# LayerNorm outputs of a fused attention and MLP block transposed by the DMA engine and modulated in place, instead of on TensorE through PSUM

One core of one Trainium2 chip. The metric is device time of one execution in microseconds (us), lower is better.

## The reference

One transformer block with adaptive modulation, bf16, 2048 tokens of 640 features, 32 heads of 20 features, MLP width 1536. Cut to what matters:

```python
mod = (silu(c) @ w_mod).reshape(1, 6, 1, 640)
sa, ca, ga, sb, cb, gb = (mod[:, i] for i in range(6))
h = layernorm(x) * (1 + ca) + sa            # "modulation"
qkv = h @ wqkv                              # ... split in 32 heads
p = softmax(q @ k.T * 20 ** -0.5)           # 2048 x 2048 for each head
x = x + ga * ((p @ v) @ wo)
h = layernorm(x) * (1 + cb) + sb
x = x + gb * (((h @ w_gate) * (h @ w_up)) @ w_down)
```

LayerNorm works on tokens in partitions, the matmuls after it need features in partitions. So each normalised tile (128 tokens x 640) has to be transposed. The scale and shift of the modulation are per feature, so after the transpose they are per partition, which one instruction does for 512 tokens.

## The kernel before

All engines' work is created as tasks with an assumed duration in ns, and a planner in the program puts them into one fixed order per engine before anything runs. `dve(195, ...)` is a VectorE task assumed to take 195 ns. `prio` is its rank among tasks that are ready in the plan (lower goes first), `dma("sp", bytes, ...)` is an entry of the one DMA queue on SyncE. At run time each engine does its list in order and waits where it must.

First LayerNorm, block `tc` of 512 tokens. Four TensorE transposes fill a PSUM bank, one eviction modulates 512 tokens of 128 features:

```python
def hT_rounds(tc, prio):
    ...
    for k in range(KD):                      # KD = 5 groups of 128 features
        mms = []
        for i in range(4):                   # 4 tiles of 128 tokens
            f = lambda e, b, i=i, k=k: e.transpose(bankh(b)[:, i * 128:(i + 1) * 128],
                                                   xn[:, s2, i, k * 128:(k + 1) * 128], ident[:])
            mms.append((C128, f))
        def after(r, k=k):                   # eviction with modulation, DVE or ACT
            ...
            f = lambda e: e.tensor_scalar(dst, bankh(r.b["b"])[:, 0:512], mcol[:, 1, k:k + 1], mcol[:, 0, k:k + 1],
                                          op0=ALU.mult, op1=ALU.add)
            return [evac(512, 455, f, fa, [r.last] + ev_col)]
        ...
```

The second LayerNorm does the same for each chunk of tokens (`h2T`, in the "suffix": output projection, LayerNorm, MLP) beside the attention of later chunks. The modulation columns are made from 25 matmuls for each vector, each one column wide:

```python
f = lambda e, b, nbk=nbk, k=k: e.matmul(ps[:, b, nbk:nbk + 1], buf[:, k, nbk * 128:(nbk + 1) * 128],
                                        scol[:, k:k + 1], start=(k == 0), stop=(k == KD - 1))
```

The exponentials run on ScalarE (line 1214) and VectorE makes the rest of the weights by adding integer constants to a linear score (`DB`, line 1238, then the shifts `DSS`, line 1252). These shifts feed the p @ v matmuls:

```python
tsx = Task("dve", 575.0, fsh, list(st_["p1"]), prio=2.5 + .001 * qi, name=f"SH.{qi}.{jj}")
```

Keys and queries reach their final layout by a round trip over the same SyncE queue: written to DRAM rows (`k_rows<-KPA`, `q_rows<-KPA`), with zeros written between the query rows (`q_rows<-Ocp`), and read back (`KT<-k_rows`, `QT<-q_rows`).

```python
q_zero[tc] = [dma("sp", 12 * H * 1024, lambda e, tc=tc: e.dma_start(..., Ocp[48:80, 1, KD - 1, :]...),
                  [z_oc[1], d_wm[4][0]], prio=9.5, dur=720.0, gate=WM_GATE + 20 + 12 * tc)]
```

The softmax here doesn't subtract the row's maximum and nothing guards it: scores larger than these inputs give would overflow.

## Time and profile before

| | before |
|---|---|
| time | 869.9 us, median of 2 (869.32 to 870.48) |
| span of the profiled run | 865.9 us, granted clock 0.992 |
| exponentials | 691, 788.3 us of ACT |
| first exponential starts, last ends | 17.28, 829.0 us |
| idle of ACT between exponentials | 23.4 us in all |
| of it in front of exponentials 1 to 10, 11 to 20, 21 to 59, 60 to 690 | 6.6, 6.3, 5.8, 4.8 us |

How to read it: exponentials are numbered from 0 in order of time. "The stall in front of exponential n" is the time from the end of exponential n-1 to the start of exponential n in the trace's records of ACT. ACT is the bound, so the time of a kernel is nearly first start + 788 us + stalls + tail, and each change can be looked for in one of these four terms. "Half clock" is time in which the granted clock of TensorE is recorded as 0.5. The prediction below shows the lines of the profile.

### The profile page before, as it was taken

How to read it: one execution, taken by the hardware profiler on the slowest of the kernel's cores; microseconds unless marked ns; L12 is line 12 of the kernel's file. 1: busy time of each engine (PE TensorE's matmuls, PEld its weight loads, DVE VectorE, ACT ScalarE, POOL GpSimd, SP SyncE). 2: the span in 40 equal slices, each digit the busy share in tenths (PEclk: the TensorE clock that was granted, in tenths of full speed). 3: DMA queues.
4: the chain of work that ended last, by engine and by line, in shares of the span. 5: the costliest groups of instructions: out<-in, count | busy, mean ns of one | idle time of the engine just before them, and what ended most of it. 6: DMA issues, size and time to landing. Idle time of an engine off the chain costs nothing.

```text
span 865.9 us, 30616 instructions
## 1 busy us (share of the span) xinstructions
PE 829.4 (96%) x13568; PEld 327.5 (38%) x13568; DVE 713.1 (82%) x1338; ACT 802.5 (93%) x718; POOL 32.0 (4%) x65
## 2 busy tenths in 40 slices
PE   8899999999999999999999999999999999999998
PEld 4433333322233322233333322223445444455577
DVE  7865888796999999999889999999779877775463
ACT  4698999999999999899999999999999999999931
POOL 2300000000001000000000100000001100000000
PEclk9997999999999999999999999999999999999999
DMA  9163331122510125110301011110310036203640
GB/s 300 38 216 94 92 86 37 29 71 76 156 29 23 33 55 146 43 24 6 66 10 44 5 36 44 44 36 2 67 50 7 21 75 139 59 21 82 136 88 18
DMA packets 118459, 56.37 MB, mean 65 GB/s; under 512 B 84439, under 2 KB 118327, under 8 KB 118327
## 3 DMA queue, kind: packets, MB, share of 16 engines
q1 hardware_dynamic: 117399, 53.26, 24.2%
q8 instruction: 107, 1.75, 0.9%
q10 hardware_dynamic: 928, 1.15, 0.4%
q14 instruction: 25, 0.20, 0.1%
HBM read 42.93 MB, written 9.16 MB: 60 GB/s over the span
## 4 chain that ended last, share of the span: by engine, by line
PE 44%; ACT 34%; DVE 15%; issue 3%; DMA 2%; POOL 1%; SPq 1%; DVEq 0%; ACTq 0%
ACT PP L1214 34%; PE ps_all L747 16%; PE ps_all L1596 13%; PE ps_all L1180 12%; DVE DB L1238 4%; DVE DSS L1252 3%; PE ps_all L914 2%; DVE st L802 1%; DMA k_rows<-KPA 1%; DVE st L1400 1%; DVE xck L1390 1%; DVE OT L1305 1%; DVE xn L1407 1%; PE ps_all L829 1%; DMA stg<-in_B_w_gate_dram 1%
## 5 line engine op out<-in xcount | busy, mean ns | idle before, releaser
L1214 ACT ACTIVATE PP<-ps_all 128x1536 bf16<-128x1536 f32 (+1 forms) x691 | 788.3, 1279 | 13.5 <-PE ps_all L1180 9.7
L1180 PE MATMUL ps_all<-QT,KT 32*128 32x512 bf16 (+1 forms) x2560 | 295.2, 341 | 14.5 <-ACT PP L1214 11.5
L1252 DVE TENSOR_SCALAR DSS<-DB 128x2048 int16<-128x2048 int16 x400 | 265.9, 683 | 20.0 <-PE ps_all L1596 17.7
L1238 DVE TENSOR_SCALAR DB<-ps_all 128x512 int16<-128x512 f32 x320 | 217.2, 682 | 38.7 <-PE ps_all L1180 37.0
L1180 PEld LDWEIGHTS ps_all<-QT,KT 32*128 32x128 bf16 x2560 | 77.2, 91 | 256.6 <-ACT PP L1214 185.7
L1596 PE MATMUL ps_all<-PP,Vf 128*32 128x512 bf16 (+3 forms) x2184 | 171.9, 344 | 1.5 <-DVE OT L1305 1.5
L1596 PE MATMUL ps_all<-DSS,Vf 128*32 128x512 bf16 (+2 forms) x1880 | 151.7, 351 | 0.0
L747 PE MATMUL ps_all<-h2T,stg 128*32 128x512 bf16 x1440 | 109.7, 381 | 2.8 <-DVE DB L1238 1.7
L1596 PEld LDWEIGHTS ps_all<-PP,Vf 128*32 128x32 bf16 (+1 forms) x2184 | 48.3, 94 | 95.3 <-issue 84.9
L1596 PEld LDWEIGHTS ps_all<-DSS,Vf 128*32 128x32 bf16 (+1 forms) x1880 | 47.8, 96 | 36.1 <-issue 16.0
L747 PE MATMUL ps_all<-wd,hprod 128*32 128x320 bf16 x1152 | 55.2, 300 | 0.4 <-DVE DB L1238 0.3
L747 PEld LDWEIGHTS ps_all<-h2T,stg 128*32 128x32 bf16 x1440 | 34.8, 96 | 35.1 <-issue 9.4
L1465 DVE CAST gsb<-ps_all 128x512 bf16<-128x512 f32 (+1 forms) x48 | 29.5, 615 | 10.8 <-PE ps_all L747 10.6
L747 PEld LDWEIGHTS ps_all<-wd,hprod 128*32 128x32 bf16 x1152 | 29.2, 96 | 14.9 <-issue 4.8
L747 PE MATMUL ps_all<-wV,hT 128*32 128x320 bf16 x640 | 32.9, 300 | 1.9 <-DVE DB L1238 0.8
L1403 POOL TENSOR_SCALAR sd<-mv 128x1 f32<-128x1 f32 x14 | 7.0, 499 | 739.7 <-DVE mv L1402 739.7
L747 PE MATMUL ps_all<-wo,Ocp 128*32 128x320 bf16 x640 | 31.9, 300 | 0.4 <-DVE xck L1390 0.3
L1596 PE MATMUL ps_all<-DB,Vf 128*32 128x512 bf16 (+2 forms) x376 | 32.1, 349 | 0.0
L1305 DVE STREAM_TRANSPOSE OT<-ps_all 128x512 f32<-128x512 f32 (+1 forms) x40 | 24.2, 605 | 8.8 <-PE ps_all L1596 8.6
L914 PE MATMUL ps_all<-hT,wk 128*32 128x512 bf16 x380 | 29.9, 381 | 0.4 <-DVE Vf L994 0.4
L914 PE MATMUL ps_all<-hT,wq 128*32 128x512 bf16 x375 | 29.0, 394 | 0.9 <-DVE Vf L994 0.3
L1476 DVE TENSOR_TENSOR hprod<-ps_all,gsb 128x512 bf16<-128x512 f32 x36 | 24.5, 681 | 5.3 <-PE ps_all L747 5.3
(107 smaller groups left out, 486.6 us busy)
## 6 DMA issues: line engine op xcount, KB each, us to landing
stg<-in_B_w_gate_dram SPq DMA_DIRECT2D x50, 160.0 KB
stg<-in_B_w_up_dram SPq DMA_DIRECT2D x50, 160.0 KB
KT<-k_rows SPq DMA_DIRECT2D x120, 32.0 KB
QT<-q_rows SPq DMA_DIRECT2D x22, 128.0 KB
wm<-in_w_mod_dram SPq DMA_DIRECT2D x3, 800.0 KB
k_rows<-KPA SPq DMA_DIRECT2D x18, 128.0 KB
x<-in_A_x_dram SPq DMA_DIRECT2D x7, 320.0 KB
xck<-in_A_x_dram SPq DMA_DIRECT2D x3, 640.0 KB
```

The source lines that it names most:

```text
L747: return lambda e, b: e.matmul(ps[32 * x:32 * x + 32, b, 0:n], lhs()[:, 32 * x:32 * x + 32], rhs(), tile_position=(0, 32 * x), start=st, s ...
L802: bns.append(dve(393, lambda e, t=t, i=i, hf=hf: e.bn_stats(st[:, i, 6 * hf:6 * hf + 6], x0[:, t, 320 * hf:320 * hf + 320]), [d_x[tc][i // ...
L829: f = lambda e, b, i=i, k=k: e.transpose(bankh(b)[:, i * 128:(i + 1) * 128], xn[:, s2, i, k * 128:(k + 1) * 128], ident[:])
L914: f = [lambda e, b_, k=k, x=x: e.matmul(ps[x:x + min(32, w - x), b_, :], wx[:, k, r0 + x:r0 + min(x + 32, w)], hT[tc][:, k, :], tile_posit ...
L1180: ems.append(lambda e, i=i, kt=kt: e.matmul(dstf()[:, i * u.n:(i + 1) * u.n], KT[32 * u.s:32 * u.s + 32, u.j, kt * 128:(kt + 1) * 128], QT ...
L1214: return e.activation(PPs[g % 2][:, cellp["p"], 0:nu * 512], ps[:, b0:b0 + nu, :].rearrange("p b c -> p (b c)"), AFT.Exp, scale=ESCALE)
L1238: return e.tensor_scalar(DB0[:, st_["slot"], x * 512:(x + 1) * 512], bank(cell["b"]), EBIAS, 0.0, op0=ALU.add, op1=ALU.max)
L1252: return e.tensor_scalar(DSS[:, cell["s"], :], DB0[:, st_["slot"], :], float(SHIFTS[jj]), None, op0=ALU.add)
L1305: t1 = Task("dve", n * 1.1 + 70, lambda e: e.transpose(OT[:, 0:n], ps[:, BPV, 0:n]), [], prio=0.0, name=f"T1.{it}")
L1465: f = lambda e: e.tensor_copy(gsb[:, gs, 0:n], ps[:, r.b["b"], 0:n])
L1476: f = lambda e: e.tensor_tensor(hprod[:, fc, 0:n], ps[:, r.b["b"], 0:n], gsb[:, gs, 0:n], ALU.mult)
L1596: ems.append(lambda e, i=i, kt=kt, stt=stt, stp=stp: e.matmul(ps[32 * s:32 * s + mc, BPV, 0:u.n], Vf[:, (kt * H + 4 * u.j + s) * VW:(kt * ...
```

## The change

Intent: take 130 transposes and 35 PSUM evictions off TensorE, VectorE and ScalarE by letting 26 DMA transposes write the transposed tile straight to SBUF, and modulate it there in place. Apart from that the column matmuls are written 64 wide, so that TensorE looks busier and its clock stays up. Block 0 and the last chunk stay on TensorE.

```diff
+DMA_T = (1, 2, 3)
+TR_BYTES = 300000
...
-                f = lambda e, b, nbk=nbk, k=k: e.matmul(ps[:, b, nbk:nbk + 1], ...
-                                                        scol[:, k:k + 1], ...
+                f = lambda e, b, nbk=nbk, k=k: e.matmul(ps[:, b, nbk * NCOL:nbk * NCOL + NCOL], ...   # NCOL = 64
+                                                        scol[:, k:k + 1].to_broadcast([128, NCOL]), ...
...
+        if tc in DMA_T:
+            for i in range(4):
+                tr_last[tc].append(dma("sp", TR_BYTES, lambda e, i=i: e.dma_start(
+                    hT[tc][:, :, i * 128:(i + 1) * 128], xn[:, s2, i, :], transpose=True), [t_xn[tc][i]], prio=0.05,
+                    dur=550.0))
+            for k in range(KD):
+                t_hT[tc].append(dve(195, lambda e, k=k: e.tensor_scalar(
+                    hT[tc][:, k, :], hT[tc][:, k, :], mcol[:, 1, k:k + 1], mcol[:, 0, k:k + 1], op0=ALU.mult,
+                    op1=ALU.add), tr_last[tc] + ev_col, prio=1))
+            return
...
+        if not tail:
+            for tl in range(ntl):
+                tr_l.append(dma("sp", TR_BYTES, lambda e, tl=tl: e.dma_start(
+                    h2T[:, :, tl * 128:(tl + 1) * 128], xn2[:, tl, :], transpose=True), ..., prio=0.05, dur=550.0))
+            for k in range(KD):
+                t_h2.append(dve(n * .265 + 60, ... in place on h2T[:, k, 0:n] ...,
+                    tr_l + [r_sb.evac[0], r_cb.evac[0]], prio=1))
-        for k in range(KD):
+        for k in range(KD if tail else 0):
...
-            sc.activity(start, 1.0 if cand.name[:3] == "col" else cand.dur * 2.37)
+            sc.activity(start, cand.dur * 2.37)
```

`dur=550.0` is the assumed time that one transpose holds the SyncE queue.

More of the change, by code (lines that the diff above doesn't have):

```diff
@@ L749, in quarters @@
         return [one(x) for x in range(4)]
-    C512, C320, C128, C1 = 216.0, 136.0, 57.0, 26.0
+    C512, C320, C128, C1 = 216.0, 136.0, 57.0, 28.0
+    NCOL = 64
     def X(n):
@@ L760, in col_round, with src @@
             for k in range(KD):
-                f = lambda e, b, nbk=nbk, k=k: e.matmul(ps[:, b, nbk:nbk + 1], buf[:, k, nbk * 128:(nbk + 1) * 128],
-                                                        scol[:, k:k + 1], start=(k == 0), stop=(k == KD - 1))
+                f = lambda e, b, nbk=nbk, k=k: e.matmul(ps[:, b, nbk * NCOL:nbk * NCOL + NCOL],
+                                                        buf[:, k, nbk * 128:(nbk + 1) * 128],
+                                                        scol[:, k:k + 1].to_broadcast([128, NCOL]),
+                                                        start=(k == 0), stop=(k == KD - 1))
                 mms.append((C1, f))
+        def src(r):
+            return ps[:, r.b["b"], 0:KD * NCOL].rearrange("p (a b) -> p a b", b=NCOL)[:, :, 0]
         def after(r):
             if plus:
-                f = lambda e: e.tensor_scalar(mcol[:, slot, :], ps[:, r.b["b"], 0:KD], 1.0, None, op0=ALU.add)
+                f = lambda e: e.tensor_scalar(mcol[:, slot, :], src(r), 1.0, None, op0=ALU.add)
             else:
-                f = lambda e: e.tensor_copy(mcol[:, slot, :], ps[:, r.b["b"], 0:KD])
+                f = lambda e: e.tensor_copy(mcol[:, slot, :], src(r))
             return [dve(75, f, [r.last], prio=0)]
@@ L1414, in suffix @@
         tr_l = []
-        for k in range(KD):
+        if not tail:
+            for tl in range(ntl):
+                tr_l.append(dma("sp", TR_BYTES, lambda e, tl=tl: e.dma_start(
+                    h2T[:, :, tl * 128:(tl + 1) * 128], xn2[:, tl, :], transpose=True),
+                    [t_xn2[tl]] + (first if alt else bd.get("h2T", []) + kv_last), prio=0.05, dur=550.0))
+            for k in range(KD):
+                t_h2.append(dve(n * .265 + 60, lambda e, k=k: e.tensor_scalar(
+                    h2T[:, k, 0:n], h2T[:, k, 0:n], mcol[:, 3, k:k + 1], mcol[:, 2, k:k + 1], op0=ALU.mult, op1=ALU.add),
+                    tr_l + [r_sb.evac[0], r_cb.evac[0]], prio=1))
+        for k in range(KD if tail else 0):
             mms = []
@@ L1506, in suffix @@
         bd["hp"] = dn_last[-1:]
-        bd["tr"] = tr_l[-1:]
+        bd["tr"] = tr_l if not tail else tr_l[-1:]
         bd["out"] = outs
```

## The prediction

> **What bounds the kernel now.** I began with the page's busy shares, then cut the span into stages by what ScalarE (ACT) does, and only then looked at the clock, the groups and the chain of waits.
>
> ```profile
> PE 829.4 (96%) x13568; PEld 327.5 (38%) x13568; DVE 713.1 (82%) x1338; ACT 802.5 (93%) x718; POOL 32.0 (4%) x65
> ```
>
> PE looks fullest, but a matmul's recorded time overlaps its neighbours', so 96% does not make PE the bound. ACT's 802.5 us are nearly all the exponentials of line 1214 (691 of them, 788.3 us), and the change removes none. So the useful question is where ACT is not running exponentials. The busy times in stretches that I cut at the first exponential (17.28), at two stalls and at the last exponential (829):
>
> ```profile
> core 0: us, PE busy (x) PEld busy (x) DVE busy (x) ACT busy (x) POOL busy (x), PEclk, DMA share, GB/s
> 0.00:17.28 17.28, 13.72 (x159) 6.89 (x163) 12.91 (x52) 5.11 (x9) 3.96 (x13) 0.90 0.97 303
> 17.28:50.00 32.72, 29.59 (x481) 13.61 (x473) 27.34 (x71) 24.70 (x25) 9.79 (x22) 1.00 0.31 89
> 50.00:77.00 27.00, 25.31 (x374) 8.62 (x372) 19.75 (x34) 26.36 (x23) 0.00 (x0) 1.00 0.59 178
> 77.00:90.00 13.00, 12.29 (x150) 4.43 (x153) 2.40 (x7) 7.66 (x7) 0.00 (x0) 0.61 0.40 102
> 90.00:829.00 739.00, 715.91 (x11402) 266.73 (x11394) 633.12 (x1133) 734.23 (x645) 16.98 (x28) 1.00 0.23 55
> 829.00:866.00 37.00, 32.60 (x1020) 27.27 (x1020) 17.54 (x45) 4.47 (x12) 1.23 (x2) 1.00 0.12 33
> ```
>
> Read the ACT column against the length of the row. From 90 to 829 us ACT idles 739.00 - 734.23 = 4.8 us: 85% of the kernel is bound by ACT and cannot give more than that. What can move is the head (17.28 us to the first exponential), 8.0 us of idleness in 17.28 to 50, 5.3 us in 77 to 90, and the tail of 37 us, which PE bounds. The granted clock in 77 to 90 is 0.61; in finer stretches:
>
> ```profile
> 10.00:11.00 1.00, 1.00 (x9) 0.76 (x9) 0.35 (x3) 0.00 (x0) 0.00 (x0) 0.50 1.08 344
> 11.00:12.00 1.00, 1.00 (x12) 1.00 (x11) 0.69 (x2) 0.67 (x1) 0.00 (x0) 0.50 1.15 310
> ...
> 76.00:78.00 2.00, 0.69 (x16) 0.43 (x16) 1.07 (x2) 0.99 (x2) 0.00 (x0) 0.95 0.23 56
> 78.00:80.00 2.00, 2.00 (x17) 0.41 (x14) 0.68 (x1) 1.45 (x1) 0.00 (x0) 0.50 0.24 73
> 80.00:82.00 2.00, 2.00 (x33) 0.95 (x32) 0.17 (x2) 1.11 (x2) 0.00 (x0) 0.50 0.95 191
> ```
>
> PE ran at half clock twice: about 9.8 to 12.9 us, and about 77.9 to 88.9 us. Both times the one-column matmuls of line 761 (the modulation columns) ran just before or during it, at 7.7 to 9.9 and at 75.9 to 83. The groups that the change touches:
>
> ```profile
> L829 PE MATMUL ps_all<-ident,xn 128*128 128x128 bf16 x80 | 7.9, 244 | 1.8 <-DVE hT L837 1.1 <-ACT hT L835 0.6
> L837 DVE TENSOR_SCALAR hT<-ps_all,mcol 128x512 bf16<-128x512 bf16 x14 | 7.4, 541 | 2.4 <-PE ps_all L829 2.3
> L835 ACT ACTIVATE hT<-ps_all,mcol 128x512 bf16<-128x512 bf16 x6 | 4.7, 778 | 8.8 <-PE ps_all L829 8.7
> L1423 DVE TENSOR_SCALAR h2T<-ps_all,mcol 128x512 bf16<-128x512 bf16 x15 | 7.7, 530 | 0.7 <-PE ps_all L1418 0.7
> L813 DVE TENSOR_SCALAR xn<-x,mv,rs 128x640 bf16<-128x640 bf16 x16 | 6.9, 433 | 0.6 <-POOL rs L811 0.5
> ```
>
> The reader should see small groups: the whole transposing path is some 30 us of work spread over three engines.
>
> **What the Trainium skill says.** (1) "VectorE: DVE Perf Modes", the perf-mode tier table: a tensor_scalar on bf16 in SBUF may run at four elements a cycle, with PSUM as source at no more than two. The trace agrees in part: line 1252 (128x2048, int16, SBUF) took 683 ns, near the fast rate, but line 813 (128x640, bf16, two per-partition scalars) took 433 ns, which fits two a cycle as well. (2) The same page, "The three transpose paths": 390 ns for a 128x128 transpose on TensorE, 1309 ns on the DMA. Here a TensorE transpose is recorded at 219 ns and a group of four occupies 0.33 us start to start. (3) "Advanced Engine Details and Errata", X-Bar Transpose: such transfers are as fast as plain ones, 350 to 400 GB/s. By (3) the 164 KB of one transfer take 0.45 us, by (2) its five blocks take 6.5 us; no run yet says which, and this is the largest doubt. (4) "TensorE: Matmul & The Clock Gate", Part 1: the clock is halved after a window of about 3.4 us with too little activity. The trace agrees: the first slow spell is 3.1 us long, the second 11 us, three such windows.
>
> **The change, part by part.**
> - Removed on PE: 60 of line 829's 80 transposes (block 0 keeps 20) and 70 of the suffixes' 80 (the last chunk keeps 10). 130 x 82 ns = 10.7 us, with 35 rounds fewer on the two PSUM banks that projections, suffix and DVE scores share. In 90 to 829 this lies beside ACT's exponentials and is worth almost nothing.
> - Removed evictions: block 0 used 3 of line 837's 14 and 2 of line 835's 6, so 11 on DVE and 4 on ACT go, with 15 + 5 of line 1423. DVE: 11 x 541 + 15 x 530 + 5 x 391 ns = 15.9 us. ACT: 4 x 778 ns = 3.1 us, but those four stand where ACT was waiting for keys anyway.
> - Added on DVE: 35 modulations in place, all SBUF. My estimate from line 1252 (683 ns less 2048 elements at the fast rate leaves 150 ns fixed) is 283 ns for 512 elements, from line 813 at the slower rate 367 ns. 30 x 0.283 to 0.367 plus 5 x about 0.22 us gives 9.6 to 12.1 us. Net on DVE: 4 to 6 us less, on an engine with room except in 15 to 35 us, where it is full.
> - Added on the DMA: 12 + 14 = 26 transposes of 160 KB on the SP queue, 4.3 MB beside 56.37 MB.
> - Latency, block by block: from the last normalised tile to the last transposed piece took 21.36 to 26.09 us in block 1, 28.05 to 32.86 in block 2, 35.16 to 40.84 in block 3: 4.7, 4.8 and 5.7 us. By DMA I estimate 0.5 (issue, as the queue's other entries) + 2.5 to 3 (a 320 KB load of x landed in 3.0) + 5 modulations of 0.28 to 0.37: 4.4 to 5.4 us. That is a draw; the gain there is what DVE and PE save around it. I take -1 us for 17.28 to 50.
> - The modulation columns written 64 wide: matmuls of line 761 start 26 ns apart already, so the wider form costs about 0.2 us for all 100, and it fills the windows with activity. If the first slow spell goes, block 0's 20 transposes need some 1.2 us where they took 2.33, and with the evictions between them the head shrinks by about 0.7 us. If the second goes, ACT's gaps there (1.34, 0.49, 0.62, 1.26, 0.16, 1.48 us, sum 5.35) fall to the first one, which was there before the clock fell: -4 us. I give that three chances in four: -3.
> - 90 to 829: at most 4.8 us to gain; I take -0.5.
> - Tail: the last chunk is unchanged. Chunk 3's transposes will be issued near 799 us among some twenty weight loads (DMA share 0.96 and 0.85 in 795 to 805), so they may land a few us late, and its gate and up matmuls start later. Against it, PE has 10 transposes less. I take +0.5.
>
> Sum: -0.7 - 1 - 3 - 0.5 + 0.5 = -4.7 us, so 869.9 - 4.7 = about 865.
>
> **The rivals.** (A) The DMA transposes are slow, as in (2). Four for block 1 would then take about 26 us instead of 2 to 3, keys for block 1 come up to 20 us late, and ACT starves in 20 to 60: 880 to 890. For it: the page's figure. Against it: the diff's own scheduler assumes under 1 us of queue for each, and someone set that number for this kernel. One in ten. (B) They are as fast as hoped but queue behind weight loads: blocks 1 and 2 behind x and projection weights (DMA share 1.08 in 15 to 20 us), chunk 3 behind its weights. That costs 2 to 8 us: 867 to 873. One in four. (C) The slow clock stays, or moves elsewhere, because the schedule is rebuilt throughout and fewer transposes mean less PE activity: then the change is a wash, 868 to 870. (D) Everything is hidden and only the schedule's accidents remain: 866 to 872. For it: ACT is 99% busy in the long stage.
>
> **Range and chances.** The centre is 865. Below, all stalls of 17 to 90 us together are 13.4 us, and taking two thirds of them gives 857. Above, rival B gives up to 874. To be 2% faster the kernel would have to end under 852.5, which needs every idle us named here outside the tail: 0.03. To be 2% slower it must pass 887.3, rival A at its worst: 0.04.
>
> **What would show it.** Right: the granted clock is 1.00 in the stretches near 10 to 12 and 78 to 89 us; ACT idles under 2 us in the stage that was 77 to 90; the sum of exponentials is unchanged at 788 us; in-place modulations of 512 elements take 280 to 370 ns; a transpose lands 2 to 4 us after its issue; blocks 1 to 3 are ready 4 to 6 us after their last normalised tile; the tail stays at 36 to 39 us. Wrong: transposes that take over 5 us each, ACT waiting on keys of block 1 or 2 for more than it did, another halved clock elsewhere, or a tail longer by over 3 us.

## More of the kernel before

Where the planner expects TensorE to stand idle, it puts in "fills", matmuls whose result nobody reads (line 1831). They are meant to keep its clock up.

## The result, and the profile after

| | before | after |
|---|---|---|
| time, median of 2 | 869.9 (869.32 to 870.48) | 894.78 (893.57 to 895.98) |
| ratio, 95% interval | | 1.0293 [1.0247, 1.034], slower |
| exponentials | 788.3 us | 788.4 us |
| first starts, tail after the last | 17.28, 36.9 | 17.35, 36.3 |
| stalls between exponentials | 23.4 | 49.7 |
| in front of 1 to 10, 11 to 20, 21 to 59, 60 to 690 | 6.6, 6.3, 5.8, 4.8 | 11.3, 8.8, 12.4, 17.2 |
| half clock, sum | 13.7 us in 2 spells | 30.7 us in 5 spells |

The head, the exponentials and the tail have not changed by more than 0.6 us. The whole loss, 26.2 us, is stalls between exponentials: +4.6, +2.6, +6.6 and +12.4 us in the four sections. The busy sums of the page and of the DMA queue do not show a bound engine. After:

```profile
PE 842.3 (94%) x13486; PEld 326.7 (37%) x13486; DVE 712.3 (80%) x1343; ACT 799.1 (90%) x713; POOL 31.3 (4%) x65
...
q1 hardware_dynamic: 134871, 57.53, 26.5%
```

and the queue's line of the kernel before (packets, MB, share of 16 engines' span):

```profile
q1 hardware_dynamic: 117399, 53.26, 24.2%
```

DVE's busy time fell by 0.8 us instead of 4 to 6. PE's rose by 12.9 us although 130 transposes went: the fills alone take 13.9 us more (below). All DMA engines worked 26.5% of 891.6 less 24.2% of 865.9 = 26.7 us more, 1.03 us for each of 26 transposes. That is small; what matters is when.

The busy times in stretches, after (columns as in the prediction, cut at the first and last exponential, at 50, 77, 90 and 120 us):

```profile
core 0: us, PE busy (x) PEld busy (x) DVE busy (x) ACT busy (x) POOL busy (x), PEclk, DMA share, GB/s
...
17.35:50.00 32.65, 23.70 (x389) 10.95 (x381) 23.82 (x69) 14.33 (x14) 10.01 (x22) 0.95 0.64 130
...
77.00:90.00 13.00, 13.00 (x216) 5.82 (x218) 7.62 (x17) 13.00 (x12) 0.00 (x0) 1.00 0.48 137
90.00:120.00 30.00, 25.84 (x227) 6.38 (x219) 14.98 (x26) 17.67 (x16) 0.00 (x0) 0.77 0.30 77
120.00:855.39 735.39, 709.10 (x11211) 262.05 (x11213) 615.97 (x1106) 718.19 (x631) 16.10 (x28) 0.99 0.24 57
```

and of the kernel before, the two stretches that answer to the last two:

```profile
90.00:120.00 30.00, 28.61 (x413) 9.46 (x409) 25.63 (x48) 30.00 (x27) 0.00 (x0) 1.00 0.38 94
120.00:829.00 709.00, 687.30 (x10993) 257.27 (x10985) 607.50 (x1087) 704.23 (x619) 16.98 (x28) 1.00 0.22 54
```

Read the ACT column against the row's length. In 17.35 to 50 ACT now idles 18.3 us, where it was 8.0. The stretch 77 to 90 is full and at clock 1.00, as the prediction had hoped, but 90 to 120 has taken its place: 12.3 us idle at clock 0.77, where the kernel before had none. After 120 us ACT idles 17.2 us instead of 4.8.

The groups that the change touches, after, and then the fills of before:

```profile
L840 DVE TENSOR_SCALAR hT<-hT,mcol 128x512 bf16<-128x512 bf16 x15 | 5.7, 442 | 3.4 <-DMA hT<-xn 3.4
L1439 DVE TENSOR_SCALAR h2T<-h2T,mcol 128x512 bf16<-128x512 bf16 x15 | 5.2, 407 | 0.7 <-DMA h2T<-xn 0.7
L1858 PE MATMUL ps_all<-ident 128*128 128x512 bf16 x96 | 32.4, 420 | 3.8 <-POOL ident L705 1.5 <-DVE DB L1256 1.3 <-DVE KPA L941 0.5
```

```profile
L1831 PE MATMUL ps_all<-ident 128*128 128x512 bf16 x48 | 18.5, 442 | 3.2 <-POOL ident L703 1.5 <-DVE DB L1238 1.0 <-ACT hT L835 0.6
```

These are means of a line; 28 of the 30 modulations are recorded at 394 to 413 ns. The recorded lengths overlap: most groups of five take 1.70 us, about 0.32 us from start to start. The other two took 693 and 685 ns. They ran beside the two memsets on GpSimd at 41.04 and 41.51 us, and the same pair is as long (685 to 694 ns) beside these memsets in early_only, no_col, early_23 and both_23_modlate below; in both_true and early_true, where the memsets meet only the last modulation and for under 0.25 us, none is. No run tests this as a cause. In line 840 VectorE stood 3.4 us on the DMA. The number of fills went from 48 to 96.

The DMA queue on SyncE, after, around block 1 (start, time in the queue, entries; the last four transposes shown are those of block 2):

```profile
19.01 1.22 SPq L836 DMA_TRANSPOSE hT<-xn  x1
...
26.44 5.16 SPq L836 DMA_TRANSPOSE hT<-xn  x4
31.65 1.97 SPq L988 DMA_DIRECT2D KT<-k_rows  x4
```

This is the clearest surprise. A transpose holds the queue for 1.2 to 1.33 us in 22 of 26 cases (the others for 1.53 to 2.79), where a plain entry holds it for 0.48 us in the median, and nine of ten for under 0.75. Four in a row are 5.2 us in which the reads of keys behind them (`KT<-k_rows`) cannot be issued. An issue alone lands in 2.6 to 2.7 us (landings are from the trace's semaphore records); in block 1 the four landed 3.15, 5.80, 6.17 and 3.85 us after their issue, in 20 to 30 us, where the DMA share is 1.31 and 1.03. From the last normalised tile to the last modulated piece, block 1 takes 21.42 to 29.94 us, block 2 26.75 to 35.40, block 3 33.79 to 43.88: 8.5, 8.7 and 10.1 us, where before it was 4.7, 4.8 and 5.7. The waits of 20 to 45 us show the way to ACT (L840 is the modulation, L880 makes keys, L890 copies them):

```profile
DVE hT L840 <- DMA hT<-xn: 3.4, 2, 2.7
ACT KT L890 <- PE ps_all L880: 5.3, 1, 5.3
```

and of the kernel before, for the same copy of keys:

```profile
ACT KT L872 <- PE ps_all L862: 1.7, 1, 1.7
```

### The profile page after: what moved, and what is told of

Same layout as the page of the kernel before. It is cut to its first block, busy times and chain, and to the rows that moved or that the text cites. A ratio compares the mean times of both kernels' runs of the same rounds, so it can differ in the third digit from the quotient of the medians. Undisturbed runs are those within 1.5% of the kernel's fastest.

```text
span 891.6 us, 30479 instructions
## 1 busy us (share of the span) xinstructions
PE 842.3 (94%) x13486; PEld 326.7 (37%) x13486; DVE 712.3 (80%) x1343; ACT 799.1 (90%) x713; POOL 31.3 (4%) x65
## 2 busy tenths in 40 slices
DMA packets 135930, 60.61 MB, mean 68 GB/s; under 512 B 101911, under 2 KB 135799, under 8 KB 135799
## 3 DMA queue, kind: packets, MB, share of 16 engines
q1 hardware_dynamic: 134871, 57.53, 26.5%
## 4 chain that ended last, share of the span: by engine, by line
PE 48%; ACT 32%; DVE 12%; issue 4%; DMA 3%; POOL 1%; SPq 0%; POOLq 0%; DVEq 0%; ACTq 0%
ACT PP L1232 32%; PE ps_all L749 16%; PE ps_all L1623 14%; PE ps_all L1198 14%; PE ps_all L932 3%; DVE DB L1256 3%; DVE DSS L1270 2%; DMA wm<-in_w_mod_dram 1%; DVE st L1418 1%; DMA hT<-xn 1%; DVE st L810 1%; DVE xck L1408 1%; DVE hT L840 1%; DVE h2T L1439 1%; DMA h2T<-xn 0%
## 5 line engine op out<-in xcount | busy, mean ns | idle before, releaser
L1232 ACT ACTIVATE PP<-ps_all 128x1536 bf16<-128x1536 f32 (+1 forms) x691 | 788.4, 1291 | 39.9 <-PE ps_all L1198 30.7
L749 PE MATMUL ps_all<-h2T,stg 128*32 128x512 bf16 x1440 | 112.2, 388 | 3.6 <-DVE DB L1256 1.6
L1623 PEld LDWEIGHTS ps_all<-DSS,Vf 128*32 128x32 bf16 x1880 | 48.0, 95 | 42.8 <-issue 17.5
L749 PEld LDWEIGHTS ps_all<-h2T,stg 128*32 128x32 bf16 x1440 | 35.6, 97 | 37.4 <-issue 11.5
L932 PE MATMUL ps_all<-hT,wk 128*32 128x512 bf16 x380 | 33.3, 415 | 4.3 <-DMA wk<-in_A_wqkv_dram 2.2
L1858 PE MATMUL ps_all<-ident 128*128 128x512 bf16 x96 | 32.4, 420 | 3.8 <-POOL ident L705 1.5
L749 PEld LDWEIGHTS ps_all<-wd,hprod 128*32 128x32 bf16 x1152 | 29.0, 96 | 18.3 <-issue 5.7
L1323 DVE STREAM_TRANSPOSE OT<-ps_all 128x512 f32<-128x512 f32 (+1 forms) x40 | 24.2, 605 | 10.9 <-PE ps_all L1623 10.8
```

The costliest lines, as they stand in the source:

```text
L749: return lambda e, b: e.matmul(ps[32 * x:32 * x + 32, b, 0:n], lhs()[:, 32 * x:32 * x + 32], rhs(), tile_position=(0, 32 * x), start=st, s ...
L932: f = [lambda e, b_, k=k, x=x: e.matmul(ps[x:x + min(32, w - x), b_, :], wx[:, k, r0 + x:r0 + min(x + 32, w)], hT[tc][:, k, :], tile_posit ...
L1232: return e.activation(PPs[g % 2][:, cellp["p"], 0:nu * 512], ps[:, b0:b0 + nu, :].rearrange("p b c -> p (b c)"), AFT.Exp, scale=ESCALE)
L1323: t1 = Task("dve", n * 1.1 + 70, lambda e: e.transpose(OT[:, 0:n], ps[:, BPV, 0:n]), [], prio=0.0, name=f"T1.{it}")
L1623: ems.append(lambda e, i=i, kt=kt, stt=stt, stp=stp: e.matmul(ps[32 * s:32 * s + mc, BPV, 0:u.n], Vf[:, (kt * H + 4 * u.j + s) * VW:(kt * ...
L1858: task.emits = [lambda e: e.matmul(ps[:, b_, :].rearrange("p (a b) -> p a b", a=4), ident[:], ident[:].unsqueeze(1).to_broadcast([128, 4, ...
```

## Experiments

The theory after the result had three parts. (i) Blocks 1 to 3 go a longer way, because a transpose costs 1.28 us of queue and waits behind loads. (ii) The suffixes' in-place modulations, five in a burst, run on VectorE ahead of the shifts that p @ v waits for. (iii) The wider columns do nothing. The main rival: it is the luck of a new fixed order, and the transposes have little to do with it. "Suffix on PE" below stands for these edits on the changed kernel:

```diff
-        if not tail:
+        if False:
...
-        for k in range(KD if tail else 0):
+        for k in range(KD):
...
-        bd["tr"] = tr_l if not tail else tr_l[-1:]
+        bd["tr"] = tr_l[-1:]
```

Times are medians of 4 runs against 7 or 8 of the kernel before on the same chip. Stalls are read from one profiled execution of each kernel.

| run | us | ratio [95%] |
|---|---|---|
| col_only | 869.91 | 1.0004 [0.9982, 1.0027] |
| no_col | 885.13 | 1.0174 [1.0142, 1.0205] |
| early_only | 882.94 | 1.0146 [1.0115, 1.0177] |
| suffix_only | 877.94 | 1.0098 [1.0071, 1.0125] |
| early_plain | 878.12 | 1.0088 [1.0056, 1.0119] |
| early_23 | 871.85 | 1.0027 [0.9997, 1.0056] |
| before_dl36 (control) | 874.88 | 1.0057 [1.0038, 1.0076] |
| suf_modlate | 870.72 | 1.0017 [0.9999, 1.0036] |
| early_1 | 878.24 | 1.0109 [1.0092, 1.0126] |
| early_qz | 876.59 | 1.0085 [1.0067, 1.0103] |
| after_modlate | 887.71 | 1.0219 [1.0201, 1.0238] |
| after_modlate_qz | 880.02 | 1.0125 [1.0097, 1.0153] |
| both_true | 878.88 | 1.0103 [1.0052, 1.0154] |
| both_23_modlate | 875.0 | 1.0048 [1.001, 1.0086] |
| before_qz (control) | 875.04 | 1.0058 [1.0012, 1.0105] |
| before_dl34 (control) | 872.26 | 1.0018 [0.9979, 1.0057] |
| suf_true | 875.9 | 1.0052 [1.0004, 1.0099] |
| early_true | 872.17 | 1.0027 [0.998, 1.0074] |

### The parts one at a time

**col_only**: the wider columns alone (`DMA_T = ()` and suffix on PE).

> The column part alone: modulation columns 64 wide and counted as PE activity, all transposes back on PE. Theory (the two DMA parts make all of the loss): within 4 us of before, 866 to 874. Step of the prediction under test: the half-clock spells near 9.5 and 77.8 us vanish and the time falls by about 4 us, 866. Rival (rebuilding the schedule by itself throws in stalls): 875 or more. Rival (the column part is to blame): near 895.

The time is unchanged. The half clock spell of 10.2 us that was at 77.8 us is at 87.5 us, as long as before, and stalls are 25.7 us instead of 23.4. The first spell stays too (3.4 us at 9.0). So the step of the prediction worth -4 us fails by itself: the spell was moved, not removed. Over all twenty kernels here, each profiled once, the first spell is there in 3 of 5 with narrow columns and in 8 of 15 with wide ones, so the width does not decide it.

**no_col**: both DMA parts, columns one wide (cut: the output slice is one wide too, and the assumed time of a column matmul is 26 ns again).

```diff
-                                                        scol[:, k:k + 1].to_broadcast([128, NCOL]),
+                                                        scol[:, k:k + 1],
...
-            sc.activity(start, cand.dur * 2.37)
+            sc.activity(start, 1.0 if cand.name[:3] == "col" else cand.dur * 2.37)
```

> The changed kernel with the one-column matmuls and their old accounting, both DMA parts kept. Theory: the loss stays, 888 to 898. If the column part is to blame: near 870.

The columns do not make the loss: the two DMA parts without them still lose 15 us. That is under the expected 888 to 898. The order came out different again, with 10.2 us of half clock instead of 30.7, and it is 9.7 us shorter than the whole change. Keep that number: it is what another order of the changed kernel is worth when no transpose and no rank is touched.

**early_only**: blocks 1 to 3 by DMA, suffix on PE, columns wide.

> DMA transposes for blocks 1 to 3 of the first LayerNorm only; the suffixes transpose on PE. Theory: the gaps between exponentials before 120 us stay (they grew by about 14.5 us from before to after), so 869.9 + 14.5 = 884, and the gaps near 303, 515 and 686 us are gone. Rival (the stalls of the suffixes are mere echoes of the head): near 895. Rival (the suffix part makes the loss): near 870.

It loses 13 us and has no new stall after 120 us (2.5 us in front of exponentials 60 to 690). The stall in front of exponential 4 is 10.8 us instead of 6.6, in front of 11 it is 7.3 instead of 6.0, and in front of 46 it is 9.2 instead of 1.5. In its profile the stalls make 11.1 us of the loss; the first start (19.03 us) and the tail (39.4) make 4.3 more. The tail runs from 34.8 to 41.1 us over the twenty kernels (41.1 in the control before_dl34), so a few us in it are the order's.

**suffix_only**: chunks 0 to 3 by DMA, all blocks on PE (`DMA_T = ()`).

> DMA transposes for the suffixes of chunks 0 to 3 only; blocks 1 to 3 transpose on PE. Theory: the head is as before (gaps of 12.6 us up to exponential 11), and the suffix stalls of together about 12 us stay: 880 to 884. Rival (suffix stalls are echoes of the head): near 870.

It loses 8 us, not the expected 10 to 14. The stalls in front of 4 and 11 are as before (6.65 and 5.99), and two new ones stand in front of 267 (4.7 us, at 344.6) and 548 (5.7 us, at 670.1). Both parts therefore cost time, at different places; 13.1 + 8.1 + 0.1 = 21.3 us of the 24.9.

### What the blocks pay for

**early_plain**: early_only with the transposing mode off, on the same order of instructions. The result is wrong: the blocks are copied untransposed. The comparison does not see a wrong first LayerNorm output; only the time is used here.

```diff
-  hT[tc][:, :, i * 128:(i + 1) * 128], xn[:, s2, i, :], transpose=True), [t_xn[tc][i]], prio=0.05,
+  hT[tc][:, :, i * 128:(i + 1) * 128], xn[:, s2, i, :].rearrange("p (k c) -> p k c", c=128)), [t_xn[tc][i]], prio=0.05,
```

> The early part alone (as early_only) with every DMA transpose replaced by an ordinary copy of the same 160 KB from SBUF to SBUF in the same place of the queue; the program's order is otherwise the same, and the result is wrong on purpose. Theory (a transpose holds the SP queue 1.28 us where a plain entry holds it 0.42 to 0.5, so four in a row cost some 3 us more per block): blocks 2 and 3 are ready about 3 us sooner, the two head gaps shrink from 10.8 + 7.3 to some 13 us in all, time 876 to 879. Rival (what hurts is waiting behind the loads of x and the weights, or the order): still 881 to 884.

The plain copies hold the queue for about 0.6 us each and give back about 5 us of 13 (the two intervals just touch). The stall in front of 11 falls from 7.3 to 3.8 us; the one in front of 4 stays at 10.0. Block 1's copies still land 3.5, 5.8, 6.2 and 6.0 us after issue. So block 1 pays for the detour over a busy DMA, whatever the mode. (The profile is of the fastest of its four runs, 873.58 us.)

**early_23**: only blocks 2 and 3 by DMA (`DMA_T = (2, 3)`, suffix on PE).

> Early part for blocks 2 and 3 only; block 1, whose transposes landed 5.8 and 6.2 us after issue among the loads, goes back to PE. Theory (block 1's wait behind the loads makes the first gap): the gap at exponential 4 returns to 6.6 us, the gap at exponential 11 stays over 6 us, time 872 to 877. Rival (any re-planned head is bad): 881 to 885.

The stall in front of 4 is exactly that of before (6.60), the one in front of 11 grows to 11.5, and the time is within 0.3% of before, just under the expected 872 to 877.

**early_1**: only block 1 by DMA (`DMA_T = (1,)`, suffix on PE).

> Only block 1 goes by the DMA; blocks 2 and 3 and every suffix are transposed on PE, columns 64 wide. If the queue behind the x loads is what block 1 pays for, the stall in front of exponential 4 is 10 to 11 us as in the two kernels that have block 1 on the DMA (6.6 where it is on PE), and the stall in front of exponential 11 goes back to at most 6 us (7.3 to 11.5 with blocks 2 and 3 on the DMA): about +4 us for that, 873 to 878 with the luck of a new plan. Rival, the plan's luck alone: the stall before exponential 4 has no tie to block 1's route and falls anywhere between 6.6 and 10, time 870 to 875.

The stall in front of 4 is 12.1 us, over the expected 10 to 11 and far from the 6.6 of block 1 on PE. Its transposes land 3.8, 6.0, 6.4 and 3.8 us after issue. The stall in front of 11 shrinks to 1.3 us, but 7.0 us appear in front of 17, so these two share one piece of work (6.3 to 8.4 us in front of 11 to 20 altogether). The time, 878.2, is just over the range, with 8.9 us in front of 46. In front of 1 to 20 block 1 alone adds 7.6 us to the 12.9 of before, and blocks 2 and 3 alone (early_23) add 5.2. The profile of early_1 is 5.0 us longer than that of early_23, but only 2.4 of these lie in front of 1 to 20, so it does not show the first block alone to be the dear one.

### The stall near 90 us

The chain of waits of the whole change in 90 to 98 us (waiting engine and line, what for, sum, times, longest):

```profile
ACT PP L1232 <- PE ps_all L1198: 7.4, 1, 7.4
...
PEld ps_all L1198 <- DMA QT<-q_rows: 3.2, 1, 3.2
```

ACT waits for scores, and the scores wait for queries to come back from DRAM. The queue in the whole change:

```profile
81.62 8.26 SPq L988 DMA_DIRECT2D KT<-k_rows  x16
89.92 1.70 SPq L975 DMA_DIRECT2D q_rows<-KPA  x3
91.66 0.41 SPq L1134 DMA_DIRECT2D q_rows<-Ocp  x1
95.29 0.82 SPq L997 DMA_DIRECT2D QT<-q_rows  x2
```

Sixteen reads of keys take the queue for 8.3 us, and only then come the rows of queries and the zeros between them. My guess was the zeros (issued at 79.0 in the kernel before). The reads and the rows of queries there:

```profile
79.53 5.06 SPq L970 DMA_DIRECT2D KT<-k_rows  x8
86.81 1.16 SPq L957 DMA_DIRECT2D q_rows<-KPA  x2
```

**early_qz**: early_only with the zeros earlier.

```diff
-            Ocp[48:80, 1, KD - 1, :]...), [z_oc[1], d_wm[4][0]], prio=9.5,
+            Ocp[48:80, 1, KD - 1, :]...), [z_oc[1], d_wm[4][0]], prio=1.45,
```

> Blocks 1 to 3 by DMA as in the run that gave 882.9, and the write of zeros that the rows of Q wait for is moved ahead of the bulk of the writes on the same queue (it was issued at 91.7 us there in the whole change, 79.0 before). If the stall near 90 us is Q waiting in that queue, 9.2 us in front of exponential 46 shrinks to under 3 and the kernel takes 870 to 876. Rival: the zeros are not what Q waits for, the stall stays at 7 to 9 us and the time within 3 us of 882.9.

Half right. The zeros were issued at 78.3 and landed at 82.5, but the rows of queries were still issued at 88.3 to 90.4, behind the keys. The stall in front of 46 shrank to 6.9 us only, and the time by 6 us to 876.6.

**before_qz**: the same edit on the kernel before, so without a single DMA transpose.

> The kernel before with the zeros ahead of the bulk of the writes: a control for the versions with that mending. If earlier zeros help by themselves, 864 to 868; if this is no more than another order, 869 to 876 as the other control (874.9).

It is 0.6% slower than before, and in front of exponential 46 it has a stall of 10.9 us, longer than any version with transposes. Its queue:

```profile
81.24 8.98 SPq L970 DMA_DIRECT2D KT<-k_rows  x16
90.27 1.73 SPq L957 DMA_DIRECT2D q_rows<-KPA  x3
92.14 0.36 SPq L979 DMA_DIRECT2D QT<-q_rows  x1
```

The same picture. So this stall does not need transposes. Over the twenty kernels it is there (4.7 to 10.9 us in front of 46) in the ten whose queue begins sixteen reads of keys in a row between 76 and 84 us. Sixteen reads alone do not make it: in early_23, both_23_modlate, both_true and early_true they begin at 66 to 69 us, the rows of queries follow at 75.7 to 78.4, and no stall in front of 40 to 50 is over 3.7 us. The transposes may still favour the late order: all eight kernels with block 1 on the DMA and planned with 550 ns have it, two of the ten with block 1 on PE, and neither of the two planned with 1280.

**before_dl36** and **before_dl34**: the kernel before with one constant moved by 0.01 (`D_LEAD = 0.36`, `D_LEAD = 0.34` for 0.35).

> A control without any DMA transpose: the kernel before with D_LEAD 0.36 in place of 0.35, which shifts by a hair when the vector engine's score tiles fall due and so re-plans everything. If the loss comes from the DMA transposes as such: within 2 us of before. Rival (the constants of the kernel before are tuned to one lucky plan, and any re-planning loses some of it): 874 to 880, with new gaps near exponential 46 or the chunk borders.

> The kernel before with the lead of the writes at 0.34 instead of 0.35: a second control for what another order costs with no transposes. The kernel before was tuned, so its neighbours should be the same or slower: 869 to 875; a neighbour at 864 would mean that 870 is nothing to keep.

The first loses 5 us and has the same sixteen reads (at 79.52, for 9.96 us) and a 9.9 us stall in front of 46. The second has the same order there as before, stalls of 22.0 us in all, and is within 0.2%. Of three neighbours of the kernel before two are thus 0.6% slower and one, like col_only, cannot be told from it. None is faster, so it may be a tuned point, and another order alone can cost some 5 us. The rival is right to that extent, and no difference of a few us between two versions below is put down to one part alone.

### What the suffixes pay for

**suf_modlate**: suffix_only with the modulations ranked behind the shifts.

```diff
-                    tr_l + [r_sb.evac[0], r_cb.evac[0]], prio=1))
+                    tr_l + [r_sb.evac[0], r_cb.evac[0]], prio=2.7))
```

> The suffix part alone with the in-place modulations behind the shifts in the vector engine's priorities (2.7 in place of 1). Theory (five modulations that fall due together push the shifts back, and the next item's matmuls wait for these): the gaps of 4.7 us at exponential 267 and 5.7 us at 548 go, 869 to 873. Rival (the gaps come from something else): 876 to 879.

The stall at 548 falls from 5.7 to 0.3 us, the one at 267 goes, and the time is that of before within its interval. So a later rank alone removes the loss of suffix_only. The edit makes another order too; that the burst is what it removes is looked at under suf_true.

**after_modlate**: the same edit on the whole change.

> The whole change with one number altered: the modulations of the suffixes rank behind the shifts of the scores on VectorE. If the burst of modulations ahead of the shifts makes the stalls at 303, 515 and 686 us (2.9 + .6, 1.5 + 1.3 + .3 and 5.1 us, with two slow spells of the clock), these go and the time falls by 8 to 12 us to 883 to 887; the stalls before 120 us stay. Rival, the transposes themselves or the DMA traffic make them: less than 4 us gained, a stall over 3 us at exponential 548 stays.

Less than expected: 7 us gained, not 8 to 12. The stalls at 515 and 686 us went (0.8 us left of the first, none of the second), but 3.9 us stay at 302 to 308, and 6.8 us of half clock with them. There, four modulations still ran ahead of the shift: in the trace they start at 299.07, after VectorE had stood 0.24 us on a transpose's landing, and the shift follows at 300.37. The likely reason, not tested: in the plan, with its 550 ns, the transpose had landed by then, and the rank only decides among what is ready in the plan, not at run time.

**after_modlate_qz**: both mendings.

> Both mendings on the whole change: modulations behind the shifts, and the zeros early. If the causes are separate they add: the stalls at 90 and after 120 us go, what is left is block 1 to 3's longer way (4 us in front of exponential 4, 0 to 3 in front of exponential 11), so 869 to 876. It beats the kernel before only if the earlier zeros also take away the stalls at 77 to 90 us that the kernel before has (5.3 us): then 866 to 869.

At 880.0 it missed its upper limit of 876. The stalls after 120 us are 6.4 us (17.2 in the whole change) and those in front of 21 to 59 are 6.7 (12.4), but 11.4 and 8.3 us stay in front of 1 to 10 and 11 to 20: the detour of blocks 1 to 3. It does not beat the kernel before.

**both_true**: the whole change, planned with what a transpose really takes in the queue. Only the plan's assumption is changed; the same 26 transposes run.

```diff
-                    dur=550.0))
+                    dur=1280.0))
...
-                    ... prio=0.05, dur=550.0))
+                    ... prio=0.05, dur=1280.0))
```

> The whole change, its fixed order made with 1.28 us per transpose in the queue (as measured) instead of 0.55. If the order's wrong idea of the transposes makes the suffix stalls, the stalls at 303, 515 and 686 us fall to under 1.5 us in all (13.4 us in the whole change) and the early ones stay within 3 us: 877 to 884. Rival, the rank of the modulations alone: the stalls over 3 us stay, 888 to 896.

This is the largest gain of a single edit: 894.8 to 878.9 us, the ratio from 1.0293 to 1.0103. The stalls in front of 60 to 690 fall from 17.2 to 7.6 us, in front of 21 to 59 from 12.4 to 4.0, and half clock from 30.7 to 10.2 us. VectorE's wait for landings in line 840 falls from 3.4 to 0.6 us. The stalls in front of 4 and 11 hardly change (9.7 and 8.5 us). That the right figure, and not one more order, gained all of this is not shown. The wait in line 840 is 0.6 us in no_col too, which was planned with 550, and no_col gained 9.7 us. Of what went, 8.3 us stood in front of 21 to 59, where the controls without transposes have anything from 5.8 to 12.5. No other control of that kind was run.

**early_true**: blocks 1 to 3 only, planned with 1280 (suffix on PE).

> Only blocks 1 to 3 by DMA, the order made with 1.28 us per transpose. The transposes land as late as before, so the stall in front of exponential 4 stays at 9 to 11 us; if the order around them was the rest of that part's 13 us, 874 to 879. Rival: the transposes' latency makes all of it, 880 to 885.

Better than expected: 872.2, within 0.8% of before at the most. The stalls in front of 4 and 11 stay (9.6 and 8.5 us), but 2.2 us in front of 60 to 690 are half of before's, and half clock is 6.8 us instead of 27.3 in early_only. Its rows of queries are issued early (from 77.75), behind sixteen reads that began at 67.64. The stalls in front of 21 to 59 fall from 13.6 to 5.2 us, most of the gain: it is the stall near 90 us that went, not the detour.

**suf_true**: chunks 0 to 3 only, planned with 1280, modulations at their first rank.

> Only chunks 0 to 3 by DMA, modulations at their first rank, the order made with 1.28 us per transpose. If the wrong cost alone made the suffixes stall (4.7 and 5.7 us with 0.55), no stall over 3 us is left after 120 us and the time is 869 to 873. Rival, the rank alone: a stall of 4 us or more stays, 876 to 880.

The rival was right here: the stall in front of 548 stays at 5.7 us, the time is 875.9. The trace shows the burst (engine, line, operation, count; ACT's idle time is in brackets):

```profile
670.98 1.70 DVE L1439 TENSOR_SCALAR h2T<-h2T,mcol 128x512 bf16<-128x512 bf16 x5
...
672.59 1.29 DVE L1270 TENSOR_SCALAR DSS<-DB 128x2048 int16<-128x2048 int16 x2
...
673.87 0.45 DVE L1323 STREAM_TRANSPOSE OT<-ps_all 128x256 f32<-128x256 f32 x1
...
674.37 0.87 PEld L1623 LDWEIGHTS ps_all<-PP,Vf 128*32 128x32 bf16 x32 [0.21 <-DVE OT L1323]
...
674.92 2.37 ACT L1232 ACTIVATE PP<-ps_all 128x1536 bf16<-128x1536 f32 x2 [5.72 <-PE ps_all L1623]
```

Five modulations hold VectorE for 1.6 us, the shift waits, the item's last p @ v and the eviction `OT` wait for the shift, the next item's p @ v waits for that, and ACT has no free buffer for its output. But the burst is 1.6 us of the 5.7. ACT stood still from 669.2, and until the burst began VectorE worked on shifts (`DSS`) and the linear score (`DB`). In suf_modlate, where ACT's exponential 547 ends at 668.34, the eviction that ends this chain ran before that:

```profile
667.55 0.43 DVE L1323 STREAM_TRANSPOSE OT<-ps_all 128x256 f32<-128x256 f32 x1
```

What VectorE does around it is another sequence altogether. So the burst is shown as a part of the stall, and the rank as a lever that removes it; the rest of the 5.7 us goes with VectorE's other work, and is not taken apart here. In the kernel before, each eviction with modulation came after four transposes of its own on PE, so five were spread over 4.2 to 10.4 us. Here each modulation waits for all the transposes of its chunk, so the last landing releases all five at once.

**both_23_modlate**: 22 of the 26 transposes, block 1 on PE, late rank (`DMA_T = (2, 3)`, `prio=2.7`).

> Blocks 2 and 3 and chunks 0 to 3 by DMA (22 of 26 transposes), block 1 on PE, modulations of the suffixes last. If block 1's route and the suffixes' order are the causes, 869 to 874, the stall in front of exponential 4 is 6.6 us and no stall over 3 us after 120 us. Rival, a share of the loss that every transpose brings: 22/26 of 25 us, 888 or more.

875.0 us is 1 us over the expected range, and 13 under the rival's 888. The stall in front of 4 is 7.4, that in front of 11 is 11.2, no stall after 120 us is over 2.6. So 22 transposes can be run for a loss of 0.5%, no more than the controls' 0.2 to 0.6%.

No version beat the kernel before. The combination of both_true with the late rank was not run.

### All twenty kernels by section

Each of these kernels has an order of its own, so what holds across them is not the luck of one. Stalls between exponentials in us, lowest to highest:

| | in front of | kernels | stalls |
|---|---|---|---|
| all blocks on PE | 1 to 20 | 8 | 12.8 to 13.7 |
| one block or more by DMA transposes | 1 to 20 | 11 | 16.0 to 21.2 |
| plain copies (early_plain) | 1 to 20 | 1 | 14.8 |
| suffix on PE | 60 to 690 | 11 | 2.1 to 5.4 |
| suffix by DMA, first rank | 60 to 690 | 5 | 7.6 to 17.2 |
| suffix by DMA, late rank | 60 to 690 | 4 | 6.3 to 8.6 |
| no transposes by DMA at all | 21 to 59 | 5 | 5.8 to 12.5 |
| some | 21 to 59 | 14 | 4.0 to 13.6 |

The first two sections part cleanly: blocks by DMA cost 2 to 8 us, and suffixes by DMA at the first rank 2 to 15 us, whatever the order. The third does not part: it goes with the order, not with the transposes alone.

## Why the prediction was wrong

It said 865 (857 to 874); the time was 894.8. By its own steps:

- **Bound and sum of exponentials: right.** 788.3 and 788.4 us; everything is in ACT's idle time.
- **"The transposes' latency is a draw", -1 us in 17 to 50: failed, and it is the step that names the wrong cost.** It took 0.5 us for the issue "as the queue's other entries" and 4.4 to 5.4 us for a block. An entry takes 1.2 to 1.33 us, mostly, and four of them share one queue. In block 2 the last is issued 3.9 us after the first; block 1's are issued between loads, 2.5 to 2.8 us apart, and landed up to 6.2 us after issue. The blocks took 8.5, 8.7 and 10.1 us. The landing of a transpose by itself, 2.5 to 3 us in the prediction, was right (2.6 to 2.7). The stalls of exponentials 1 to 20 grew by 7.2 us. By early_plain the transposing mode is about 5 us of early_only's 13, and the rest comes with the detour or the order.
- **"90 to 829: at most 4.8 us to gain; I take -0.5": failed worst.** The prediction counted the busy time of VectorE and saw slack; it did not ask in which order VectorE serves modulations and shifts. Stalls from exponential 60 on grew by 12.4 us. suf_modlate removes the suffix part's loss by rank alone. suf_true shows that the right duration alone doesn't. The other 6.6 us of new stalls are in front of 21 to 59, where the scores waited for queries near 90 us and the prediction had expected a gain.
- **Columns, -3, and head, -0.7: failed.** col_only is 1.0004. The spell of 10.2 us moved from 77.8 to 87.5 us, as rival C said of "moves elsewhere"; the first spell stayed. (The record of the clock has the spells of before at 9.5 for 3.4 us and at 77.8 for 10.2, not 3.1 and 11 as the prediction read them.)
- **In-place modulation at 283 to 367 ns: nearly right in effect.** Recorded 394 to 413 ns but for two, about 320 ns from start to start. DVE's saving of 4 to 6 us became 0.8 us; no run shows either to be worth anything.
- **Tail, +0.5: small, as said, but the other sign.** 36.9 to 36.3 us.
- **The low end of the range rests on a wrong sum.** Two thirds of 13.4 us taken from 869.9 give 861, not 857.
- **Rival A: no.** The longest holds the queue for 2.79 us, and none takes over 6.2 us to land. **Rival B: right in kind** (block 1 behind loads), with 2 to 8 us the right size for that part. It lacked the transposes' own time in the queue.
- **What none of the rivals contained**: the order is fixed from assumed durations, and the assumption for the new operation was wrong by 0.65 us or more in each of 26 places. C and D name the rebuilt schedule, but give it no more than 872. The prediction even used that assumption as evidence ("someone set that number for this kernel"). The kernel planned with 1280 is 16 us faster; how much of that is the figure and how much another order is open.

What is shown and what is not: that the blocks' detour and the suffixes' modulations at the first rank each cost time is shown, across all orders tried. In the profile of the whole change the three sections grew by 7.2, 6.6 and 12.4 us. How these divide further is not shown, because every edit brings another order: early_only and suffix_only sum to 21, with 1280 early_true and suf_true sum to 8.5, and controls without any transposes move by 2.6 to 5.4 us. The stall near 90 us comes from the queue's order and needs no transpose, since before_qz has it too. The 16 us of both_true are measured, but their cause is not shown.

## What to carry to other kernels

Before moving work to a DMA queue, count what one entry holds that queue for, and how many stand in a row ahead of transfers that somebody waits for; the time to land is only half of it. In a kernel with a fixed order, give the planner the measured duration of a new operation before judging the operation, and run controls that reorder without changing anything, of the new kernel too, so that you know how much luck weighs. Where work that used to trickle out of one engine now arrives all at once, try a later rank for it than for whatever the bound engine is waiting for.

## What the Trainium skill lacked or had wrong

- "Advanced Engine Details and Errata", X-Bar Transpose, says that transposes are as fast as regular DMAs, at 350 to 400 GB/s. In landing the runs agree: a transpose of 128x640 bf16 from SBUF to SBUF landed 2.6 to 2.7 us after issue, a plain copy of the same 164 KB 2.44 us (early_plain, 30.13 us). In the queue they differ: 1.2 to 1.33 us against about 0.6. The packets of a transpose that was alone ran from 1.18 to 2.11 us after issue (276.04 us), which is some 176 GB/s for one of this size.
- "VectorE: DVE Perf Modes", The three transpose paths, gives 1309 ns for a 128x128 block on the DMA. Five such blocks in one transfer landed 2.6 us after issue, including the 1.2 to 1.3 us in the queue, so the figure must not be multiplied by blocks.
- No page gives in time what a DMA transpose holds the issuing queue for on this chip, 1.2 to 1.33 us here. The nearest is a table on "DMA: Bandwidth & Descriptors" in sequencer cycles (SBUF to SBUF: 262,144 for 8,192 tiles on previous generations).
- "DMA: Bandwidth & Descriptors" asks for at least 512 B in a transfer for full rate. The 26 transposes added 17,472 packets under 512 B (84,439 to 101,911), 672 for each, 640 of them of 256 B. The plain copies of early_plain go in packets of 256 B too, so no run here shows what the size costs.
- "VectorE: DVE Perf Modes", the perf-mode tier table, allows four elements a cycle for bf16 in SBUF. In-place modulations of 512 elements with two per-partition scalars came out at about 0.32 us from start to start, recorded at 394 to 413 ns; no run here separates the rate from the fixed part.
